# Chunked attention with a gated feed-forward block: upper words of w_in rounded ahead of the addition, first lower products a step later, another order of the beginning

## The chip, the cores and the metric

The kernel runs on one core of one Trainium2 chip. The metric is the time of one execution on the device in microseconds (us); the median of three runs before the change is 371.02 us (370.95 to 371.22). TensorE is called PE here, VectorE DVE, ScalarE ACT, GpSimd POOL and SyncE SP, as in the profile.

## What is computed

Inputs are `q`, `k`, `v` of 4 x 8 heads x 768 x 64, eight memory keys and values a head, and four weights of a gated block.

```
scores = scale * q_c @ [mem_k, k_ctx].T        # chunks of 32 queries, 16 keys left, 8 right
a = exp(scores - max); out = (a / sum(a)) @ [mem_v, v_ctx]
h = relu(x @ w_in)                             # x: the heads side by side, 4 x 768 x 512; w_in 512 x 1024
u, v = h[..., :512], h[..., 512:]
v_s = w_spatial @ normalised(v) + b_spatial
result = (u * v_s) @ w_out
```

All is float32. Every large product is made of three products of rounded words: a matrix is split in an upper word (rounded to fp32r) and a lower word (what is left), and upper x upper, lower x upper and upper x lower are added in PSUM.

## The kernel before, in words

**Attention** goes in 24 units of 128 queries (four chunks of 32), six units a batch, over all eight heads. For unit i: ACT copies the unit's keys into `kmain` (L422), PE makes the scores (L437, `sx<-kmain,q`, called s(i) here), DVE takes the maxima (L494) and subtracts (L498), ACT takes the exponential (L503), DVE sums and inverts (L508, L509, L511, called the denominators), PE transposes (L525), ACT copies (L528, `pT`), PE multiplies with the values (L437, `sx<-vmain,pT`, called a(i), which serves unit i-1 and writes the second half of the tile `sx` of s(i)), DVE scales (L477, `xs`), PE transposes (L541), ACT rounds to the upper word of `x` (L546) and DVE makes the lower word (L550). There is one buffer of `sx`.

**w_in** arrives as float64 words in eight chunks of 128 rows x 512 columns, called w0 to w7 (w0 to w3 are the right half, for `v`; w4 to w7 the left half, for `u`). Of each chunk: ACT scales the high part (L883), DVE shifts and puts the sign in (L892, L893), ACT scales the low part (L888), POOL adds the two in place in the tile `st` (L898, the addition), ACT rounds to the upper word `win_h` (L912), and DVE or POOL subtracts that from `st` for the lower word `win_l` (L916).

**First layer:** `group` (L579 to L581) makes one PSUM tile in four steps, one for each 128 rows of w_in, three products a step. The first group is for the 128 tokens of unit 0. `v` tiles have 512 columns, `u` tiles 384. ACT takes the relu (L603, L641); for `v` DVE takes the statistics (L607, L609, L611). PSUM holds three such tiles.

**Order.** Every piece of work is an operation with a number. `Plan.order` makes a list of them, and `emit` then moves single operations behind others by the table `MOVES`; each engine runs its operations in the order of that list, and what it waits for follows from who wrote or read a tile last in that same list. So a move can also turn a wait round: where rounding stands behind the addition in the list it reads the sum, and where it stands ahead, it reads the tile before the sum is written into it and the addition waits for it. `IDLES` puts idle matmuls of the identity (L277, into a PSUM tile that nobody reads) behind given operations, each 128 x 128 in two instructions. `order` itself puts one more behind a gap that it foresees.

**Loads** stand on SP's queue (L306) in a fixed order: `q`, `k` of units 0 and 1, w0, values, w1 to w3, `q`, `k` of units 2 and 3, values, w4, values, w5 to w7, values, `q`, `k` of units 4 and 5. A load waits for an earlier one by a pace that `transfer` sets, and for the buffer that it fills.

Of the kernel before, what the change touches and what calls it, by code (L numbers as in the profile page):

```python
# [37 lines left out]
)  # L38
IDLES = ((87, 5), (92, 4), (95, 2), (104, 29), (132, 1))
# [7 lines left out]
class Plan:  # L47
# [123 lines left out]
    def emit(self):  # L171
# [5 lines left out]
        for n in order:  # L177
            self.ops[n][2]()
            if n in idles:
                self.idle(idles[n])  # L180
# [3 lines left out]
def tile_chunked_attention_gmlp(  # L184
# [22 lines left out]
    nc = tc.nc  # L207
# [890 lines left out]
```

## Time and profile before

| | |
|---|---|
| median of 3 runs | 371.02 us |
| the profiled execution | 369.22 us |
| its span, first to last instruction | 367.4 us |
| PE busy | 354.0 us (96%) |
| DVE busy | 288.8 us (79%) |
| ACT, POOL busy | 186.2 us (51%), 155.8 us (42%) |
| granted clock of PE | 0.9 or more in every slice of the page |

A timeline row gives the start in us, the duration in us, the engine, the line, the operation with what it writes and reads, its size and count, and in square brackets the idle time of the engine ahead of it with what ended it. A row with several instructions gives the time from the first to the last. PE's durations overlap: the next matmul starts before the last one's end.

### The profile page before, as it was taken

Reading aid. Unit: us, or ns where it says so; the run is one execution under the profiler, and the core shown is the slowest. Engines: PE = TensorE matmul, PEld = TensorE weight load, DVE = VectorE, ACT = ScalarE, POOL = GpSimd, SP = SyncE. Lnnn points to the kernel's source line nnn. Section 1 sums busy time; section 2 is a strip of 40 time slices with the busy share of each in tenths; the row PEclk is TensorE's granted clock in tenths of the full one; section 3 lists DMA queues with packets and bytes.
Section 4 is the critical chain, followed back from the end, with each engine's and each line's share of the span. In section 5 each row is a group of like instructions: output and inputs, shape, how many; then the busy total and the mean of one; then the engine's idle time right before and its main releaser. Section 6 shows DMA issues by size and latency. Waiting matters only on the chain.

```text
span 367.4 us, 11909 instructions
## 1 busy us (share of the span) xinstructions
PE 354.0 (96%) x5026; PEld 328.2 (89%) x5026; DVE 288.8 (79%) x480; ACT 186.2 (51%) x334; POOL 155.8 (42%) x154
## 2 busy tenths in 40 slices
PE   2899999999999999999999999999999999999995
PEld 2787888988988989889889899999999999999995
DVE  3799977669659589485598697898899995997793
ACT  3668553645555355554383447346524742753361
POOL 6254643366377057820024184931295034304330
PEclk9999999999999999999999999999999999999999
DMA  8999988884797894978553619304730582230015
GB/s 210 272 234 247 218 266 251 260 259 145 223 253 208 230 268 158 250 169 286 185 167 115 242 70 337 139 1 144 235 140 2 185 242 90 79 123 15 2 43 172
DMA packets 47557, 65.52 MB, mean 178 GB/s; under 512 B 4496, under 2 KB 38928, under 8 KB 47504
## 3 DMA queue, kind: packets, MB, share of 16 engines
q1 hardware_dynamic: 46848, 64.44, 59.1%
q8 instruction: 39, 0.64, 0.8%
q10 hardware_dynamic: 656, 0.33, 0.3%
q14 instruction: 14, 0.11, 0.1%
HBM read 45.88 MB, written 18.87 MB: 176 GB/s over the span
## 4 chain that ended last, share of the span: by engine, by line
PE 87%; DMA 5%; DVE 4%; ACT 2%; issue 1%; SPq 0%; ACTq 0%
PE y L729 23%; PE f L729 16%; PE f L579 12%; PE f L580 11%; PE f L581 11%; PE sx L437 9%; DMA k<-in_k_dram 3%; PE pt L525 3%; PE xt L541 3%; DMA vmain<-in_v_dram 2%; DVE st L893 1%; DVE st L892 1%; DVE p L498 1%; DVE mx L494 1%; DVE ve L611 0%
## 5 line engine op out<-in xcount | busy, mean ns | idle before, releaser
L729 PE MATMUL y<-wsp,op 128*128 128x384 f32 x288 | 52.2, 336 | 0.0
L729 PEld LDWEIGHTS y<-wsp,op 128*128 128x128 f32 x288 | 49.9, 188 | 0.0
L579 PE MATMUL f<-x,win_h 128*128 128x384 f32 x128 | 45.9, 359 | 0.0
L783 POOL TENSOR_TENSOR ug<-st,ug 128x384 f32<-128x384 f32 x24 | 34.7, 1461 | 20.8 <-DVE st L775 16.7
L581 PE MATMUL f<-x,win_h 128*128 128x384 f32 x128 | 43.1, 337 | 0.0
L580 PE MATMUL f<-x,win_l 128*128 128x384 f32 x128 | 43.0, 336 | 0.0
L789 POOL TENSOR_TENSOR st<-st,bias 128x384 f32<-128x384 f32 x14 | 17.2, 1233 | 58.0 <-ACT st L769 39.1
L579 PE MATMUL f<-win_h,x 128*128 128x512 f32 x96 | 41.1, 428 | 0.0
L729 PE MATMUL f<-wsp,op 128*128 128x384 f32 x216 | 39.6, 336 | 0.0
L580 PE MATMUL f<-win_h,x 128*128 128x512 f32 x96 | 38.1, 397 | 0.6 <-DVE x L550 0.2
L709 DVE TENSOR_TENSOR op<-sm,op 128x768 fp32r<-128x768 f32 x32 | 34.7, 1087 | 4.0 <-ACT op L706 3.6
L581 PE MATMUL f<-win_l,x 128*128 128x512 f32 x96 | 37.6, 392 | 0.0
L729 PEld LDWEIGHTS f<-wsp,op 128*128 128x128 f32 x216 | 37.6, 188 | 0.0
L729 PE MATMUL y<-wout,op 128*128 128x256 f32 x288 | 35.8, 279 | 0.0
L615 POOL TENSOR_TENSOR rstd<-ve,mhalf 128x1 f32<-128x1 f32 x24 | 14.3, 598 | 49.6 <-DVE ve L611 49.2
L477 DVE TENSOR_TENSOR xs<-sx,rec 128x512 f32<-128x512 f32 x24 | 16.5, 688 | 23.8 <-PE sx L437 23.8
L729 PEld LDWEIGHTS y<-wout,op 128*128 128x128 f32 x288 | 34.8, 188 | 0.0
L706 ACT CAST op<-sm 128x768 fp32r<-128x768 f32 x32 | 26.4, 838 | 14.5 <-DVE sm L692 13.8
L437 PEld LDWEIGHTS sx<-kmain,q 64*32 64x32 f32 x1536 | 17.1, 107 | 14.0 <-issue 11.4
L603 ACT ACTIVATE st<-f 128x512 f32<-128x512 f32 x24 | 14.4, 598 | 28.5 <-PE f L581 28.1
L437 PE MATMUL sx<-kmain,q 64*32 64x64 f32 x1536 | 21.1, 227 | 7.2 <-ACT kmain L422 7.2
L416 POOL COPY vmain<-memv 8x1024 f32<-8x1024 f32 x22 | 23.9, 1090 | 9.8 <-PE sx L437 7.6
(86 smaller groups left out, 776.4 us busy)
## 6 DMA issues: line engine op xcount, KB each, us to landing
vmain<-in_v_dram SPq DMA_DIRECT2D x48, 128.0 KB
u_far<-uo SPq DMA_DIRECT2D x32, 192.0 KB
vn_far<-st SPq DMA_DIRECT2D x24, 256.0 KB
vr<-vn_far SPq DMA_DIRECT2D x8, 768.0 KB
ug<-u_far SPq DMA_DIRECT2D x16, 384.0 KB
q<-in_q_dram SPq DMA_DIRECT2D x11, 512.0 KB
vmain<-in_v_dram SPq DMA_DIRECT2D x47, 96.0 KB
out_dram<-ot SPq DMA_DIRECT2D x33, 128.0 KB
```

What stands on the lines that cost most here:

```text
L416: ins = {"DVE": nc.vector, "POOL": nc.gpsimd}[eng].tensor_copy(to, of)
L437: ins = nc.tensor.matmul(o, w_, m, start=True, stop=True, skip_group_check=True)
L477: nc.vector.tensor_tensor(xs.rearrange("p t r d -> p r t d"), t_["sx", i][:, :, 1], rec.rearrange("p t r -> p r t").unsqueeze(3).broadcast ...
L579: nc.tensor.matmul(o, lh, rh, start=(j == 0), stop=False)
L580: nc.tensor.matmul(o, ll, rh, start=False, stop=False)
L581: nc.tensor.matmul(o, lh, rl, start=False, stop=(j == len(pairs) - 1))
L603: nc.scalar.activation(alloc("st", s, [P, DH], F32), t_["f", n], AF.Relu)
L706: nc.scalar.copy(half(0), of())
L709: nc.vector.tensor_tensor(half(1), of(), half(0).bitcast(F32), op=ALU.subtract)
L729: nc.tensor.matmul(o, x, y, start=first and m == 1, stop=m == 3 * chunks, skip_group_check=True)
L783: nc.gpsimd.tensor_tensor(g, t_[st(x)], g, op=ALU.mult)
L789: {"DVE": nc.vector, "POOL": nc.gpsimd}[eng].tensor_tensor(a, a, bias[:, 1], op=ALU.add)
```

## The change

`LOWER` says at which step of the first group (`n == 0`) the products with the lower words `win_l` are made: none at the first step, that of w0 at the second, that of w1 at the third, those of w2 and w3 at the fourth. The twelve products of the group stay the same, the order in which they are added changes. The idle matmuls may now be small (32 columns, 64 rows), and 41 of `IDLES` become 33 large and 8 small ones. `MOVES` gets some 90 more pairs ahead of the old ones, all for operations of the first 45 us. Every other line is the same, moved by 10 to 16 lines.

```diff
 MOVES = (
-    (1035, 934), (1027, 975), (1036, 941), (1028, 948), (1037, 1028), (1038, 1037), (963, 951), (964, 950),
...
+    (22, 21), (23, 22), (24, 23), (25, 24), (32, 25), (39, 32), (11, 39), (86, 85), (87, 86), (88, 87), (89, 88),
...
-IDLES = ((87, 5), (92, 4), (95, 2), (104, 29), (132, 1))
+IDLES = ((87, (5, 128)), (95, (5, 128)), (104, (4, 128), (5, 128)), (102, (14, 128)), (594, (8, 32)))
...
+LOWER = ((), (0,), (1,), (2, 3))
...
-        idles = dict(IDLES)
+        idles = {n: how for n, *how in IDLES}
         for n in order:
             self.ops[n][2]()
-            if n in idles:
-                self.idle(idles[n])
+            for how in idles.get(n, ()):
+                self.idle(*how)
...
-    def busy(k):
-
-        for _ in range(k):
-            nc.tensor.matmul(idle, ident, ident, start=True, stop=True)
+    def busy(k, w):
+        for j in range(k):
+            if w < P:
+                c = j % 4 * w
+                nc.tensor.matmul(idle[c:c + w, 0:w], ident[0:64, 0:w], ident[0:64, 0:w], start=True, stop=True)
+            else:
+                nc.tensor.matmul(idle[:, 0:P], ident, ident, start=True, stop=True)
...
-                nc.tensor.matmul(o, lh, rl, start=False, stop=(j == len(pairs) - 1))
+                for i in (LOWER[j] if n == 0 else (j,)):
+                    lh, _, _, rl = pairs[i]()
+                    nc.tensor.matmul(o, lh, rl, start=False, stop=(i == len(pairs) - 1))
```

**ACT around the copies of the keys of units 2 and 3.** Before, `st_333`, `st_266`, `st_391`, `st_400` are the tiles of w1, w0, w2, w3 and `big_282` the words of w3:

```order
L912 CAST win_h_108<-st_333 128x512
L883 ACTIVATE st_400<-big_282 128x512
L888 ACTIVATE big_282<-big_282 128x512
L912 CAST win_h_108<-st_266 128x512
L912 CAST win_h_108<-st_391 128x512
L422 COPY kmain0_147<-k_384 128x20x32
L422 COPY kmain1_148<-k_384 128x20x32
L912 CAST win_h_108<-st_400 128x512
L503 ACTIVATE p_464<-p_464 128x512
```

Now, `st_344`, `st_346`, `st_372` are those of w1, w2, w3, and `big_176`, `big_178` the words of w2 and w3 (w0 is rounded far ahead of this):

```order
L928 CAST win_h_108<-st_344 128x512
L904 ACTIVATE big_176<-big_176 128x512
L542 COPY pT_383<-pt_353 128x512
L928 CAST win_h_108<-st_372 128x512
L436 COPY kmain0_147<-k_377 128x20x32
L928 CAST win_h_108<-st_346 128x512
L436 COPY kmain1_148<-k_377 128x20x32
L904 ACTIVATE big_178<-big_178 128x512
L517 ACTIVATE p_442<-p_442 128x512
```

The rounding of w2 and the low part of w3 now stand behind the first copy of the keys.

**DVE from the maxima of unit 2 on.** Before (`win_l_109<-st_400` is the lower word of w3, `st_508` is w4, `stats_606` the statistics of the first group):

```order
L494 TENSOR_REDUCE mx_459<-sx_419 128x8
L498 TENSOR_TENSOR p_464<-sx_419,mx_459 128x2x4x64
L916 TENSOR_TENSOR win_l_109<-st_400,win_h_108 128x512
L477 TENSOR_TENSOR xs_504<-sx_419,rec_338 128x2x4x64
L508 TENSOR_REDUCE den_518<-p_464 128x8
L509 TENSOR_TENSOR den_518<-den_518,eps_103 128x8
L511 RECIPROCAL rec_521<-den_518 128x8
L892 TENSOR_SCALAR st_508<-st_508 128x512
L893 SCALAR_TENSOR_TENSOR st_508<-big_405,st_508 128x512
L607 BN_STATS stats_606<-st_568 128x6
```

Now (`st_346` is w2, `st_372` w3, `st_506` w4):

```order
L508 TENSOR_REDUCE mx_440<-sx_405 128x8
L512 TENSOR_TENSOR p_442<-sx_405,mx_440 128x2x4x64
L932 TENSOR_TENSOR win_l_109<-st_346,win_h_108 128x512
L932 TENSOR_TENSOR win_l_109<-st_372,win_h_108 128x512
L491 TENSOR_TENSOR xs_523<-sx_405,rec_391 128x2x4x64
L908 TENSOR_SCALAR st_506<-st_506 128x512
L909 SCALAR_TENSOR_TENSOR st_506<-big_398,st_506 128x512
L522 TENSOR_REDUCE den_533<-p_442 128x8
L523 TENSOR_TENSOR den_533<-den_533,eps_103 128x8
L525 RECIPROCAL rec_536<-den_533 128x8
L623 BN_STATS stats_603<-st_514 128x6
```

The lower word of w2, which stood ahead of the maxima, now stands behind the subtraction, so that one more operation lies between the maxima of unit 2 and the statistics of the first group.

**PE from s(2) on.** Before:

```order
L437 MATMUL sx<-kmain_147,q 32x64 x32
L579 MATMUL f<-win_h,x 128x512
L580 MATMUL f<-win_h,x 128x512
L581 MATMUL f<-win_l,x 128x512
L579 MATMUL f<-win_h,x 128x512
L580 MATMUL f<-win_h,x 128x512
L581 MATMUL f<-win_l,x 128x512
L437 MATMUL sx<-vmain,pT 32x64 x32
```

Now:

```order
L451 MATMUL sx<-kmain_147,q 32x64 x32
L593 MATMUL f<-win_h,x 128x512
L594 MATMUL f<-win_h,x 128x512
L593 MATMUL f<-win_h,x 128x512
L594 MATMUL f<-win_h,x 128x512
L597 MATMUL f<-win_l,x 128x512
L593 MATMUL f<-win_h,x 128x512
L594 MATMUL f<-win_h,x 128x512
L597 MATMUL f<-win_l,x 128x512
L451 MATMUL sx<-vmain,pT 32x64 x32
```

s(2) still stands ahead of the first product, and three steps of the first group instead of two stand ahead of a(2).

**DVE at the addition of w6.** Before, `st_615`, `st_642`, `st_679` are the tiles of w5, w6, w7 and `big_506`, `big_524` the words of w6 and w7:

```order
L916 TENSOR_TENSOR win_l_109<-st_615,win_h_108 128x512
L892 TENSOR_SCALAR st_642<-st_642 128x512
L893 SCALAR_TENSOR_TENSOR st_642<-big_506,st_642 128x512
L508 TENSOR_REDUCE den_688<-p_649 128x8
L509 TENSOR_TENSOR den_688<-den_688,eps_103 128x8
L511 RECIPROCAL rec_691<-den_688 128x8
L607 BN_STATS stats_703<-st_664 128x6
L609 BN_AGGR mvar_705<-stats_703 128x2
L611 TENSOR_TENSOR ve_707<-mvar_705,eps_103 128x1
L892 TENSOR_SCALAR st_679<-st_679 128x512
L893 SCALAR_TENSOR_TENSOR st_679<-big_524,st_679 128x512
```

Now `st_632`, `st_668`, `st_665` are those of w5, w6, w7 and `big_490`, `big_495` the words of w6 and w7:

```order
L932 TENSOR_TENSOR win_l_109<-st_632,win_h_108 128x512
L908 TENSOR_SCALAR st_668<-st_668 128x512
L909 SCALAR_TENSOR_TENSOR st_668<-big_490,st_668 128x512
L908 TENSOR_SCALAR st_665<-st_665 128x512
L909 SCALAR_TENSOR_TENSOR st_665<-big_495,st_665 128x512
L623 BN_STATS stats_694<-st_670 128x6
L625 BN_AGGR mvar_696<-stats_694 128x2
L627 TENSOR_TENSOR ve_698<-mvar_696,eps_103 128x1
L932 TENSOR_TENSOR win_l_109<-st_668,win_h_108 128x512
L522 TENSOR_REDUCE den_762<-p_649 128x8
```

The shifts of w7 now stand right behind those of w6; before, the denominators and the statistics stood between them.

## Rows read from the trace of the kernel before

**Rows 1.** Waits of PE, whole span: who waited for whom, us, times, longest.

```profile
PE sx L437 <- ACT kmain L422: 7.2, 3, 6.7
...
PE sx L437 <- ACT uo L641: 0.3, 1, 0.3
```

**Rows 2.** Busy time by stretch: length, engines, granted clock, DMA share, GB/s.

```profile
23.20:42.90 19.70, 18.97 (x392) 15.03 (x392) 18.49 (x35) 13.18 (x24) 9.64 (x10) 1.00 1.00 231
...
48.80:367.40 318.60, 314.70 (x4199) 294.56 (x4199) 249.98 (x409) 156.37 (x284) 129.73 (x121) 1.00 0.55 169
```

**Rows 3.** Chain of waits, 23 to 50 us: the two loads ahead of s(4).

```profile
28.75 6.89 DMA vmain<-in_v_dram
...
35.65 6.49 DMA k<-in_k_dram
```

**Rows 4.** Waits of SP's queue, 16 to 24 us.

```profile
SPq L306 <- DMA k<-in_k_dram: 2.1, 1, 2.1
```

**Rows 5.** Timeline of SP at the end of that wait.

```profile
22.44 0.30 SPq L306 DMA_DIRECT2D vmain<-in_v_dram  x1
```

**Rows 6.** Timeline of PE, 6 to 50 us.

```profile
7.84 2.36 PE L277 MATMUL idle<-ident 128*128 128x128 f32 x10
...
11.41 1.06 PE L277 MATMUL idle<-ident 128*128 128x128 f32 x8
13.10 0.85 PE L437 MATMUL sx<-vmain,pT 64*32 64x64 f32 x64 [0.63 <-DVE st L893]
...
16.41 6.64 PE L277 MATMUL idle<-ident 128*128 128x128 f32 x58
23.23 0.86 PE L437 MATMUL sx<-kmain,q 64*32 64x64 f32 x64 [0.18 <-ACT kmain L422]
...
42.94 0.86 PE L437 MATMUL sx<-kmain,q 64*32 64x64 f32 x64 [0.32 <-ACT kmain L422]
...
48.76 0.89 PE L437 MATMUL sx<-vmain,pT 64*32 64x64 f32 x64 [0.34 <-ACT uo L641]
```

**Rows 7.** Timeline of ACT, 9 to 49 us: a rounding, the copies of the keys.

```profile
21.82 0.62 ACT L912 CAST win_h<-st 128x512 fp32r<-128x512 f32 x1 [0.47 <-POOL st L898]
22.45 1.35 ACT L422 COPY kmain<-k 128x640 f32<-128x640 f32 x2
...
42.16 1.35 ACT L422 COPY kmain<-k 128x640 f32<-128x640 f32 x2 [2.50 <-DMA k<-in_k_dram]
```

**Rows 8.** Timeline of POOL, 9 to 49 us.

```profile
23.84 1.69 POOL L898 TENSOR_TENSOR st<-st,big 128x512 uint32<-128x512 uint32 x1 [0.63 <-DVE st L893]
...
34.66 1.29 POOL L916 TENSOR_TENSOR win_l<-st,win_h 128x512 fp32r<-128x512 f32 x1
```

**Rows 9.** Timeline of DVE, 16 to 49 us.

```profile
22.11 1.65 DVE L893 SCALAR_TENSOR_TENSOR st<-big,st 128x512 uint32<-128x512 uint32 x1
...
25.00 0.69 DVE L498 TENSOR_TENSOR p<-sx,mx 128x512 f32<-128x512 f32 x1
26.21 0.69 DVE L916 TENSOR_TENSOR win_l<-st,win_h 128x512 fp32r<-128x512 f32 x1 [0.53 <-ACT win_h L912]
...
27.42 0.68 DVE L508 TENSOR_REDUCE den<-p 128x8 f32<-128x512 f32 x1
...
28.46 0.38 DVE L892 TENSOR_SCALAR st<-st 128x512 uint32<-128x512 uint32 x1
...
29.51 0.69 DVE L607 BATCH_NORM_STATS2 stats<-st 128x6 f32<-128x512 f32 x1
...
30.93 0.68 DVE L550 TENSOR_TENSOR x<-xt,x 128x512 fp32r<-128x512 f32 x1
...
35.40 1.11 DVE L916 TENSOR_TENSOR win_l<-st,win_h 128x512 fp32r<-128x512 f32 x1 [0.21 <-ACT win_h L912]
...
46.27 0.69 DVE L508 TENSOR_REDUCE den<-p 128x8 f32<-128x512 f32 x1 [0.16 <-ACT p L503]
...
47.96 0.69 DVE L494 TENSOR_REDUCE mx<-sx 128x8 f32<-128x512 f32 x1
```

38 rows, old and new, of the table MOVES are left out of this document.

## The prediction

> **What bounds the kernel now.** I read the table of busy times first, then PE's waits, then busy time by stretch, then the timelines of the stretch that the diff touches.
>
> PE is busy for 354.0 of 367.4 us, so the end moves only if PE starts its unbroken run at another time, or if that run gets other work. From 48.8 us on PE is busy for 314.70 of 318.60 us [rows 2]. The operations there stand in the same order in both kernels, so nothing there is a term of the sum. PE's waits name the keys: 7.2 us in three waits for the copies into `kmain`, 6.7 of them at the start [rows 1]. What is left of them are 0.18 us ahead of s(2) and 0.32 us ahead of s(4); the last wait ahead of the run is 0.34 us at a(5), which starts at 48.76 [rows 6]. The question is how a(5) moves.
>
> Two things set it. The first is the **loads**. From 23.2 to 42.9 us the DMA engines are busy with a share of 1.00 [rows 2], and the chain into s(4) is two loads end to end, values to 35.64 and keys from 35.65 to 42.14 [rows 3]; ACT copies these keys at 42.16 [rows 7]. The keys of units 2 and 3 let SP go on at 22.44 after a wait of 2.1 us [rows 4, 5], ACT copies them at 22.45 [rows 7], s(2) starts at 23.23 [rows 6]. The second is **DVE**, busy for 18.49 of 19.70 us between s(2) and s(4), nearly as full as PE with 18.97 [rows 2]. At a(5) the profile names ACT's relu (L641, 0.3 us) [rows 1], but DVE's maxima L494 of unit 5 end at 47.96 + 0.69 = 48.65, just ahead of 48.76 [rows 6, 9], and a(5) writes the tile whose scores those maxima read. I take DVE as the later one.
>
> **Ahead of s(2).** The idle matmuls go from 82 large instructions to 66 and 16 small ones, and most of the steps of w0 to w3 are sorted anew. All of it ends at s(2), which waits for keys that land at 22.44. The loads stand in the same order on SP with the same waits, so this part costs 0 at s(2); its cover is the wait for the keys, and without it each idle instruction that is left would cost 114 ns (6.64 / 58) [rows 6]. The lower word of w1, ahead of the maxima on DVE, has to be through by 24.3; the shifts of w2 and w3 that took 1.65 us instead of 0.69 there [rows 9] now come earlier. Cost 0.
>
> **The gain side.** Between s(2) and a(2) there is one step more on PE, which fills time that PE stood there. The twelve products are the same twelve. Two idle instructions ahead of the first step of the second group go, 0.23 us at 114 ns. The eight small ones are new in the first `u` tile: two instructions each, at the 13 ns of a small matmul of s(2) (0.86 / 64) 0.2 us, at 114 ns 1.8 us [rows 6]. They are nearest to the former and lie ahead of s(4), where PE waited 0.32 us for the keys: 0, and 0.2 if that cover is gone. None of this can bring s(4) ahead of its keys. Behind s(4) PE runs the same operations, so the whole change can gain at most the wait at a(5): **0.34 us**, which gives 370.7.
>
> **The loss side.** Rounding w2 now waits behind the first copy of the keys on ACT, and POOL's addition of w2 waits for the rounding, since it overwrites what the rounding reads. Queued behind it on POOL is the addition of w3; who waits for both is DVE's two lower words.
>
> - One copy ends at 22.45 + 1.35/2 = 23.12, the rounding (0.62) ends at about 23.75 [rows 7].
> - POOL's addition starts then. One took 1.69 us while DVE worked on a lower word; a subtraction of the same size took 1.29 without such company ahead of it [rows 8]. DVE is at the maxima and the subtraction of unit 2 here, and the subtraction kept its 0.69 us beside the addition that ran from 23.84 [rows 8, 9]. So I take 1.29: w2 to 25.05, w3 to 26.35.
> - DVE ends the subtraction at 25.69 [rows 9]. The lower word of w2 comes next, while POOL is in the middle of w3. At 35.40 the same operation met POOL's of 34.66: it took 1.11 and ended at 36.51, 0.56 behind POOL's end of 35.95 [rows 8, 9]. Here it then ends at 26.35 + 0.56 = 26.91 and the next starts 0.09 earlier, as at 36.42: **26.82**.
> - The next is the lower word of w3, which started at 26.21 before [rows 9]. From it to the end of the lower word of `x` (31.61) the list holds the same operations in both kernels: lower word, `xs`, the denominators (1.04, 27.42 to 28.46), the shift of w4 (1.05), the statistics (1.42, 29.51 to 30.93) [rows 9], now with the shift ahead of the denominators. So all of it moves by 26.82 - 26.21 = **+0.61 us**.
>
> Bounds of this term: if the lower word of w2 isn't held up at all, the sum of w3 is still there only at 26.35, and DVE is 0.14 later than before; if both additions take 1.69, it is 0.61 + 0.80 = 1.41. I take 0.61, since the row at 35.40 is the same pair of operations in the same phase.
>
> Then the same DVE operations follow up to the maxima of unit 5. DVE has two idle gaps on the way, 0.21 at 35.40 and 0.16 at 46.27 [rows 9]; both are waits for ACT, which follows DVE there, so I let them stay. If both absorbed their length, 0.24 of the 0.61 would be left. The keys at 42.16 don't help: the maxima of unit 4 were already waiting for DVE and not for s(4). The 0.34 us at a(5) is no cover either, since it is DVE that ends it. Sum: a(5) from 48.76 to about 49.37, the profiled execution from 369.22 to 369.8. The median of before is 1.80 us above that execution; I carry the difference over: 371.02 + 0.6 = **371.6**.
>
> SP is moved past as well: the loads of w5 to w7 wait for buffers that POOL's additions free. The third of them is issued ahead of the values load of 28.75 [rows 3], and the addition of w3 ends at 26.35 by the above: 2.4 us of cover, cost 0; cut off, each microsecond would be one at s(4).
>
> [...]
>
> **The rivals.**
> 1. *The delay doesn't reach PE.* The gaps absorb it, or the lower word of w2 isn't held up and a(5) gains part of its 0.34 us: 370.7 to 371.2. For it: the profile names ACT at a(5). Against: DVE has 1.2 us of idle time in nearly 20. Chance 0.15.
> 2. *A second collision, slower.* Its place is POOL's addition of w6 against DVE's shift of w7, which now stands right behind the shift of w6; before, denominators and statistics lay between. If ACT's low part of w6 ends before DVE starts L909 of w7 (L893 before), POOL gets in first and L909 waits. The row at 22.11 gives the price, 1.65 - 0.69 = 0.96 [rows 9]: 371.6 + 0.96 = 372.6. Against: ACT is busy enough there that its low part may well come later. Chance 0.20.
> 3. *PE's clock falls.* [...] Now the run at 11.41 goes, so that PE stands still from there to about 13.10, 1.7 us where the longest wait was 0.63, and 28 idle instructions ahead of s(2) replace 58 and end, at 114 ns each, about 1.6 us ahead of it. [...] Chance 0.06.
> 4. *The keys come earlier*, because the new order frees a buffer or paces a load sooner than the list shows; s(2) or s(4) then starts some 1 us ahead: 370.0. Against it stands the DMA share of 1.00 [rows 2]. Chance 0.06.
>
> **How the numbers follow.** 371.6 has 0.53, with its own range from 371.2 (+0.14 to +0.24) to 372.0 (one of the two additions at 1.69). A measurement of this kernel can tell about 0.2%, 0.74 us, from no change. Faster, below 370.3: rival 4, 0.06. Within: rival 1 and most of the forecast, 0.15 + 0.45 = 0.60. Slower, above 371.76: rivals 2 and 3 and the upper end of the forecast, 0.20 + 0.06 + 0.08 = 0.34. The range runs from the 0.34 us of gain to rival 2, 370.7 to 372.6, and leaves out rivals 3, 4 and the far side of 2.
>
> **What the changed profile would show.** Right: copies of keys at 22.4 and 42.2 as before; POOL's additions of w2 and w3 at 23.8 and 25.1; DVE's first L932 after the subtraction 1.1 to 1.4 us long, ending at 26.9; the lower word of `x` ending at 32.2; a(5) at 49.4. Wrong: copies of the keys elsewhere (rival 4, and the sum has no ground); a lower word of 0.69 at 25.6 (the term is 0.14 or less); a(5) at 48.8 or before with DVE's chain later (rival 1, the bound was ACT); an L909 of some 1.65 us behind w6 (rival 2); the granted clock under 1 at s(2) (rival 3).

## The result, and the profile after

The changed kernel takes 373.74 us (median of 22 runs) against 371.37 for the kernel before (22 runs). The ratio is 1.0053 with a 95% interval of 1.0031 to 1.0075: slower by 2.0 us (1.2 to 2.8); the difference of the means is 1.6 (0.7 to 2.5). Ratios, differences of means and their intervals, here and below, leave out the runs that took over 1.5% longer than the fastest of their kernel; medians and counts take in all. The forecast was 371.6 with a range of 370.7 to 372.6, so the direction is right and the size is not.

The profiled execution of the changed kernel has a span of 370.1 us, 2.7 more than before. (The profiled one of before, 369.22 us, was faster than all but one of the 156 other runs of that kernel, so what is measured against it is measured against a good run.) The timeline of PE from a(1) to a(5):

```profile
13.37 0.85 PE L451 MATMUL sx<-vmain,pT 64*32 64x64 f32 x64 [1.16 <-DMA vmain<-in_v_dram]
...
19.03 3.29 PE L291 MATMUL idle<-ident 128*128 128x128 f32 x28
23.74 0.86 PE L451 MATMUL sx<-kmain,q 64*32 64x64 f32 x64 [1.43 <-ACT kmain L436]
...
44.34 0.85 PE L451 MATMUL sx<-kmain,q 64*32 64x64 f32 x64 [0.41 <-issue]
...
50.78 0.96 PE L451 MATMUL sx<-vmain,pT 64*32 64x64 f32 x64 [1.00 <-ACT uo L657]
```

These rows answer to [rows 6]. a(5) starts 2.02 us later (48.76 before), which accounts for most of the 2.7. PE now stands 1.43 us ahead of s(2) (0.18 before) and 1.16 ahead of a(1) (0.63 before). The stretch behind a(5) is 0.7 us longer (319.3 against 318.6); in the profiles below it varies from 318.5 to 325.9 with waits that the profile calls issue, and I leave that 0.7 open.

ACT's copy of the keys of units 2 and 3, against [rows 7]; POOL's additions of w2 and w3, of w6, and a copy of values at the end, against [rows 8]:

```profile
22.97 0.72 ACT L436 COPY kmain<-k 128x640 f32<-128x640 f32 x1 [0.87 <-DMA k<-in_k_dram]
```

```profile
24.29 2.58 POOL L914 TENSOR_TENSOR st<-st,big 128x512 uint32<-128x512 uint32 x2 [3.40 <-ACT win_h L928]
...
38.88 1.36 POOL L914 TENSOR_TENSOR st<-st,big 128x512 uint32<-128x512 uint32 x1 [1.75 <-ACT big L904]
...
48.45 1.04 POOL L430 COPY vmain<-memv 8x1024 f32<-8x1024 f32 x1
```

DVE against [rows 9]: the two lower words, the scaling behind them, the shift of w7, the scaling ahead of s(4), the denominators and the maxima ahead of a(5):

```profile
25.98 2.05 DVE L932 TENSOR_TENSOR win_l<-st,win_h 128x512 fp32r<-128x512 f32 x2
27.95 0.68 DVE L491 TENSOR_TENSOR xs<-sx,rec 128x512 f32<-128x512 f32 x1
...
39.12 1.68 DVE L909 SCALAR_TENSOR_TENSOR st<-big,st 128x512 uint32<-128x512 uint32 x1
...
43.55 0.69 DVE L491 TENSOR_TENSOR xs<-sx,rec 128x512 f32<-128x512 f32 x1
...
48.50 1.02 DVE L523 TENSOR_TENSOR den<-den,eps 128x8 f32<-128x8 f32 x1
...
49.99 0.69 DVE L508 TENSOR_REDUCE mx<-sx 128x8 f32<-128x512 f32 x1
```

The keys came 0.52 us later. Counted from their copy, the scaling stands at 4.98 us; in the kernel before it was 26.82 - 22.45 = 4.37. That is the +0.61 that the prediction has. L909 of w7 takes 1.68 us, and the denominators' small addition behind POOL's copy 1.02: so there were further collisions. Counted from the copy of the keys, a(5) stands at 27.81 us, and at 26.31 before: of the 2.02, 0.52 is the keys' and 1.50 comes behind their copy.

The run list holds something that this one profile does not show: 16 of the 22 runs have a mean granted clock of PE of 0.9965 or less and take 374.8 us (median); the other six, the profiled one among them, take 371.9.

### The profile page after: what moved, and what is told of

It reads as the page before. It is cut to its first block, busy times and chain, and to the rows that moved or that the text cites. A ratio compares the mean times of both kernels' runs of the same rounds, so it can differ in the third digit from the quotient of the medians.

```text
span 370.1 us, 11910 instructions
## 1 busy us (share of the span) xinstructions
PE 352.6 (95%) x5026; PEld 326.5 (88%) x5026; DVE 287.3 (78%) x480; ACT 186.5 (50%) x334; POOL 154.2 (42%) x154
## 4 chain that ended last, share of the span: by engine, by line
PE 88%; DMA 6%; DVE 3%; ACT 1%; issue 1%; SPq 1%; ACTq 0%
PE y L745 23%; PE f L745 16%; PE f L593 13%; PE f L594 12%; PE f L597 12%; PE sx L451 8%; DMA big<-in_moe_w_in_dram 3%; PE xt L555 3%; PE pt L539 2%; DMA k<-in_k_dram 2%; SPq L320 1%; DVE win_l L932 1%; DVE ve L627 0%; DMA out_dram<-st 0%; DVE x L564 0%
## 5 line engine op out<-in xcount | busy, mean ns | idle before, releaser
L745 PEld LDWEIGHTS y<-wsp,op 128*128 128x128 f32 x288 | 49.9, 188 | 0.1
L657 ACT ACTIVATE uo<-f 128x384 f32<-128x384 f32 x32 | 15.6, 492 | 24.1 <-PE f L597 18.1
```

What stands on the lines that cost most here:

```text
L657: op("ACT", act(HT), lambda: nc.scalar.activation(alloc("uo", i, [P, HT], F32), t_["f", n], AF.Relu), r=[("f", n)], w=[("uo", i)], rank=rank)
L745: nc.tensor.matmul(o, x, y, start=first and m == 1, stop=m == 3 * chunks, skip_group_check=True)
```

## The experiments

Three theories stood against each other. D: DVE's collisions with POOL make a(5) late. K: the new order brings the keys late. C: PE's clock falls, since the change leaves PE idle ahead of a(1) and s(2). The table counts every run of a kernel, twelve a version; "low" is the number of runs whose mean granted clock is 0.9965 or less. The difference is that of the means, against 20 to 35 runs of the kernel before taken at the same time, with a 95% interval from resampling the runs. The last column is a(5) in the profile, counted from the copy of the keys of units 2 and 3.

| kernel | low | median us | mean, less the kernel before | a(5) less keys |
|---|---|---|---|---|
| before, all runs beside the others | 32 of 134 | 371.54 | | 26.31 |
| changed, first 22 runs | 16 of 22 | 373.74 | +1.57 (0.7 to 2.5) | 27.81 |
| again (changed) | 6 of 12 | 372.55 | +0.81 (-0.1 to 1.7) | 29.11, clock low |
| idle_cut | 10 of 12 | 373.63 | +1.90 (1.0 to 2.8) | 30.23, clock low |
| idle_late | 2 of 12 | 372.54 | +0.82 (0.3 to 1.4) | 27.83 |
| idle_first | 1 of 12 | 372.59 | +1.13 (0.3 to 2.1) | 28.02 |
| idle_back | 7 of 12 | 378.09 | +5.54 (4.4 to 6.6) | 27.81 |
| w2_early | 4 of 12 | 372.63 | +0.24 (-0.6 to 1.1) | 27.80 |
| w7_apart | 5 of 12 | 372.19 | -0.36 (-1.3 to 0.5) | 28.54, late keys |
| mend | 4 of 12 | 373.08 | +0.77 (-0.3 to 1.7) | 26.69 |
| mend_all | 2 of 12 | 371.16 | -0.51 (-1.4 to 0.4) | 26.19 |
| lower_only | 4 of 12 | 371.48 | -0.52 (-1.5 to 0.6) | 27.57, late keys |
| before_gap | 2 of 12 | 372.07 | +0.30 (-0.7 to 1.3) | 26.95 |
| before_cut | 10 of 12 | 372.49 | +1.27 (0.1 to 2.4) | 27.24, clock low |
| before_both | 12 of 12 | 373.38 | +0.80 (-0.3 to 2.0) | 27.18, clock low ahead of s(2) |
| before_w2 | 1 of 12 | 372.13 | +0.62 (-0.3 to 1.5) | 26.90 |
| before_w7 | 3 of 12 | 370.83 | -0.53 (-1.7 to 0.7) | 26.09 |

"Late keys" marks profiles in which the keys of units 4 and 5 are copied more than 21 us behind those of units 2 and 3 (19.7 before) and s(4) starts 0.1 us behind their first copy, so that they and not DVE set it. (In idle_cut they are copied 21.35 us behind, but s(4) starts 1.6 us after that copy.) All four profiled runs that are low, again, idle_cut, before_cut and before_both, have their stretch of low clock between 16 and 30 us (down to 0.57 over 2 us in before_cut, to 0.50 in the other three); in the other 13 the granted clock is 1.00 in every stretch from 14 to 30 us and from 48.8 to 367.4.

### The changed kernel again, and its clock

**again** is the changed kernel with nothing edited.

> The changed kernel a second time, nothing edited. Its first profile had the keys of units 2 and 3 copied at 22.97 us (22.45 in the kernel before), the scaling behind DVE's two lower words at 27.95 (26.82), DVE's L909 of w7 1.68 us long, a(5) at 50.78 (48.76) and a mean granted clock of 0.999; over its 22 runs the clock lay between 0.990 and 1.000. Theory D (DVE's chain: two collisions with POOL, 0.6 and 1.0 us, and 0.5 us from the keys): both collisions again, the scaling 4.98 us behind the copy of the keys, a(5) between 50.2 and 50.8. Theory K (the new order brings the keys late): the copy again at 22.9 or later; if it was chance, at 22.3 to 22.7. Theory C (PE's clock falls because PE stands idle for 1.43 us ahead of s(2)): the runs with a mean clock of 0.995 or less are the majority and take some 2 us more than those at 0.999 and 1.000, and a profile of such a run shows the low stretch right behind 23 us.

Half of its runs were low, and the mean of its runs is 0.8 us above the kernel before, where the first 22 had 1.6. a(5) came at 53.55 us, where 50.2 to 50.8 was expected. Its profile is of a low run. ACT's copy of the keys and PE's s(2), then busy time by stretch (the last three numbers are the granted clock, the DMA share and GB/s):

```profile
24.44 0.72 ACT L436 COPY kmain<-k 128x640 f32<-128x640 f32 x1 [1.85 <-DMA k<-in_k_dram]
```

```profile
25.22 1.19 PE L451 MATMUL sx<-kmain,q 64*32 64x64 f32 x64 [2.64 <-ACT kmain L436]
```

```profile
22.00:24.00 2.00, 0.58 (x6) 0.38 (x4) 1.93 (x5) 0.59 (x1) 0.00 (x0) 1.00 1.09 196
24.00:26.00 2.00, 0.78 (x58) 0.79 (x63) 0.13 (x1) 1.56 (x3) 0.24 (x1) 0.70 0.84 183
26.00:28.00 2.00, 2.00 (x33) 1.54 (x20) 1.52 (x3) 0.94 (x3) 2.00 (x2) 0.50 1.00 172
28.00:30.00 2.00, 2.00 (x69) 1.38 (x68) 1.47 (x2) 0.76 (x2) 0.31 (x1) 0.95 0.93 203
```

The keys were copied 1.5 us later than in the first profile, PE was busy for 0.58 of the 2 us ahead, and its granted clock is 0.70 from 24 to 26 us and 0.50 from 26 to 28. s(2) takes 1.19 instead of 0.86 us, and a(5) comes 1.3 us later than at full clock, counted from the keys. The clock is back at 0.95 from 28 to 30 us, after PE worked through the 2 us ahead.

Theory K is not borne out as a rule of the order: over all 17 profiles the copy of the keys lies between 21.59 and 24.44 us, the order of the loads being the same in all, and both the earliest (mend) and the latest (again) belong to the changed order. The mean is 23.11 in the seven profiles built on the kernel before and 23.11 in the ten built on the changed one; 22.45, from which the prediction reckoned, is the earliest of the seven.

**idle_cut** and **idle_late** move twelve idle instructions between the run ahead of s(2) and the small ones later, the count kept:

```diff
-IDLES = ((87, (5, 128)), (95, (5, 128)), (104, (4, 128), (5, 128)), (102, (14, 128)), (594, (8, 32)))
+IDLES = ((87, (5, 128)), (95, (5, 128)), (104, (4, 128), (5, 128)), (102, (8, 128)), (594, (14, 32)))    # idle_cut
+IDLES = ((87, (5, 128)), (95, (5, 128)), (104, (4, 128), (5, 128)), (102, (20, 128)), (594, (2, 32)))    # idle_late
```

> The changed kernel, the count of idle instructions kept, twelve of them moved the other way: 16 ahead of s(2) instead of 28, so that the run ends at about 20.9 us and PE stands for 2.4 us or more ahead of s(2). Theory C: 9 or more of 12 runs below 0.9965, median 374 to 375, and in the profile a granted clock near 0.8 in the stretch from 20 to 30 us. Theory D: no change from the changed kernel, full clock in half of the runs or more.

> The changed kernel with as many idle instructions as it has, twelve of them moved: the run ahead of s(2) has 40 instead of 28 and ends at about 23.7 us instead of 22.3, and 4 small ones are left behind the first step of the u tile instead of 16. So far the changed kernel had a mean granted clock of 0.9965 or less in 22 of 34 runs (median 374.7 us; 371.9 in the others), the kernel before in 7 of 35 (374.7; 370.9). Theory C (PE's clock falls where PE stands idle for long ahead of s(2), longer when the keys land late): 2 to 4 of 12 runs below 0.9965, the median down by 1 to 2 us to about 372. Theory D (DVE's chain alone, and the clocks a matter of the chip's hour): the share stays at half to two thirds and the median at 372.5 to 373.7. Theory I (idle instructions more or fewer shift PE's later instructions and it waits for those, which cost the version with 34 more of them 5 us): nothing of that here, since the count is kept; PE's waits for issue behind 50 us stay at a few tenths.

Ten of 12 were low with the shorter run, 22 of 34 as changed, 2 of 12 with the longer one. In the profile of idle_cut PE stood 3.21 us ahead of s(2):

```profile
18.76 1.95 PE L291 MATMUL idle<-ident 128*128 128x128 f32 x16
23.92 1.18 PE L451 MATMUL sx<-kmain,q 64*32 64x64 f32 x64 [3.21 <-ACT kmain L436]
```

In idle_late it stood for 0.70 us, though the keys came later than in the first profile:

```profile
18.80 4.63 PE L291 MATMUL idle<-ident 128*128 128x128 f32 x40
24.13 0.86 PE L451 MATMUL sx<-kmain,q 64*32 64x64 f32 x64 [0.70 <-ACT kmain L436]
```

So in this order the number of idle matmuls ahead of s(2) decides in how many runs the clock falls. It also sets the time: the mean of idle_cut is 1.08 us above that of idle_late (0.3 to 1.9), and both were run at the same time. idle_cut's median of 373.6 lies just under the expected 374 to 375. But idle_late stays 0.82 us above the kernel before (0.3 to 1.4) with hardly a low run: theory C does not make the whole difference.

**idle_first** leaves the run ahead of s(2) at 28 and puts ten large instructions into the gap ahead of a(1), where the kernel before had eight:

```diff
+IDLES = ((87, (5, 128)), (92, (5, 128)), (95, (5, 128)), (104, (4, 128), (5, 128)), (102, (14, 128)), (594, (3, 32)))
```

> The changed kernel with the count of idle instructions kept and ten of the sixteen small ones replaced by ten large ones in the earlier gap, between the first transposes and a(1), where PE stood for 1.2 to 1.7 us and where the kernel before had eight. The run ahead of s(2) stays at 28. Theory C1 (only the gap right ahead of s(2) counts): 6 or more of 12 runs below a mean clock of 0.9965, as the changed kernel (22 of 34). Theory C2 (what PE did earlier counts too, since the kernel before with a gap of 1.8 us ahead of s(2) fell in only 2 of 12): 1 to 4 of 12, median 371.5 to 372.5.

One of 12 was low. For the clock, filling the earlier gap does as much as filling the later one; the median of 372.6 is at the upper end of what was expected.

**before_gap, before_cut** and **before_both** give the gaps to the kernel before (with the lines of the change that read `IDLES` and make small instructions, left out here):

```diff
-IDLES = ((87, 5), (92, 4), (95, 2), (104, 29), (132, 1))
+IDLES = ((87, (5, 128)), (92, (4, 128)), (95, (2, 128)), (104, (22, 128)), (132, (1, 128)), (594, (7, 32)))    # before_gap
+IDLES = ((87, (5, 128)), (92, (4, 128)), (95, (2, 128)), (104, (15, 128)), (132, (1, 128)), (594, (14, 32)))   # before_cut
+IDLES = ((87, (5, 128)), (95, (2, 128)), (104, (22, 128)), (132, (1, 128)), (594, (11, 32)))                   # before_both
```

> The kernel before with its run of idle matmuls ahead of s(2) cut from 58 to 44 instructions, so that it ends at about 21.4 us instead of 23.05, and 14 small ones behind the first step of the u tile (the count is kept). Theory C: 6 or more of 12 runs below 0.9965 and a median 1 to 2.5 us above the kernel before. Theory D: the clocks as in the kernel before, the time within 0.3 us of it.

> The kernel before with its run of idle matmuls ahead of s(2) cut from 58 to 30 instructions, so that it ends at about 20 us and PE stands for some 3 us ahead of s(2); 28 small ones behind the first step of the u tile keep the count. Theory C: 9 or more of 12 runs below 0.9965, the median 2 us or more above the kernel before, and in the profile a low granted clock from s(2) on, with a(5) 2 us or more later at the same landing of the keys. If the order and not PE's gap makes the clock fall: no more than 4 of 12.

> The kernel before with both of the changed kernel's gaps on PE and nothing else of it: the eight idle instructions between the first transposes and a(1) gone, the run ahead of s(2) cut from 58 to 44, and 22 small ones behind the first step of the u tile that keep the count. With the second gap alone 2 of 12 runs fell below a mean clock of 0.9965; the changed kernel with the first gap filled fell in 1 of 12, with neither filled in 22 of 34. Theory C2 (the two gaps together make the clock fall): 6 or more of 12 below 0.9965, the median 1 us or more above the kernel before. If something else of the new order is needed: no more than 3 of 12.

The expectation for before_gap failed: with only the later gap (1.78 us ahead of s(2) in its profile, at full clock) 2 of 12 were low and the time did not move clear of noise. A much longer one made 10 of 12 low, but the median came 1.0 us above the kernel before and a(5) 0.9 later, where 2 us were expected of both. The two gaps together made 12 of 12 low, as expected; the time rose by 0.8 us, with an interval that holds zero (-0.3 to 2.0). In the profile of before_both the clock is low between the two places, not behind the second:

```profile
16.00:18.00 2.00, 2.00 (x10) 2.00 (x11) 1.90 (x5) 1.08 (x3) 0.00 (x0) 0.50 0.98 295
18.00:20.00 2.00, 2.00 (x14) 2.00 (x14) 1.14 (x3) 2.00 (x4) 1.29 (x1) 0.66 0.89 267
```

There idle matmuls take the loss: the run of 44 took 5.87 us instead of the 5.08 of before_gap, and s(2) waited for the keys all the same (0.35 us), so this fall cost nothing there. a(5) is 0.87 us later by another wait, which before_gap has too, without a low clock: PE's products break off at 31 us, in before_gap put down to issue and in before_both to an operation of ACT on other data, and DVE's scaling waits for them. before_gap first, then before_both:

```profile
31.49 0.32 PE L440 MATMUL sx<-kmain,q 64*32 64x64 f32 x8 [1.27 <-issue]
```

```profile
32.64 0.69 DVE L480 TENSOR_TENSOR xs<-sx,rec 128x512 f32<-128x512 f32 x1 [0.60 <-PE sx L440]
```

```profile
32.15 0.85 PE L440 MATMUL sx<-vmain,pT 64*32 64x64 f32 x64 [1.53 <-ACT big L891]
```

```profile
33.06 0.69 DVE L480 TENSOR_TENSOR xs<-sx,rec 128x512 f32<-128x512 f32 x1 [0.70 <-PE sx L440]
```

So in before_both the gaps are shown to make the clock fall, and what the falls cost is not. In the profile of again it was the products behind s(2) that took the loss (4.01 us from s(2) to a(2), 2.83 in the changed kernel's first profile). In which share of the runs the clock falls at which place the runs don't tell, since only a profiled one has the clock by stretch. Within one version low runs have a mean some 2 us above the others (changed kernel 2.1, kernel before 2.4); loads that land late in them may be a part of that.

**idle_back** was the first try at filling both gaps, with 104 idle instructions instead of 82 (22 more; a later expectation says 34, a slip):

```diff
+IDLES = ((87, (5, 128)), (92, (5, 128)), (95, (5, 128)), (104, (4, 128), (5, 128)), (102, (20, 128)), (594, (8, 32)))
```

> The changed kernel with idle matmuls in the two gaps that it leaves on PE: ten more instructions between the first transposes and a(1), and forty in place of 28 ahead of s(2), which should end at about 23.7 instead of 22.3. Theory C: nearly all runs at a clock of 0.999 or 1.000, and the median falls by 1 to 2 us against the changed kernel in the same call. Theories D and K: a(5) stays at 50.2 to 50.8 and the times stay within 0.5 us of the changed kernel's.

It lost 5.3 us, far behind the place of the edit. Its profile has waits of PE in the middle of a row of products, put down to nothing but issue:

```profile
179.25 0.60 PE L539 MATMUL pt<-ident,p 128*128 128x128 f32 x4 [1.07 <-issue]
...
184.61 0.33 PE L451 MATMUL sx<-vmain,pT 64*32 64x64 f32 x11 [2.01 <-issue]
```

idle_late, with the same run of 40 ahead of s(2) but the count kept, has 0.7 and 0.4 us of such waits and not this loss, and neither has mend_all below, with both gaps filled and the count kept. So the loss goes with the number of PE's instructions ahead of that place (104 idle ones against 82). The expectation, nearly all runs at full clock, failed too: 7 of 12 are low with both gaps filled. The profiled run is not one of them, and where the clock falls in them stays open. Why PE waits for issue there no run shows.

### DVE's collisions, one by one

**before_w2** puts the order of w2 alone into the kernel before, with the deferred lower products (the loop that reads `LOWER` is left out here); **lower_only** has the deferred products and nothing else:

```diff
+LOWER = ((), (0,), (1,), (2, 3))                                                    # lower_only, before_w2
-    (1499, 1505),
+    (1499, 1505), (44, 41), (20, 19), (37, 114), (36, 37), (43, 36), (38, 119),     # before_w2
```

> The kernel before with the one edit that the products with the lower words in the first group come a step later (none, w0, w1, w2 and w3); order and idle matmuls as before. All theories: within 0.4 us of the kernel before, since the same twelve products stand between s(2) and the statistics of the first group; a share of runs below 0.9965 like that of the kernel before.

> The kernel before with the lower products a step later and with that part of the new order that holds back w2: the rounding of w2 behind the first copy of the keys on ACT, POOL's additions of w2 and w3 behind it, the lower word of w2 behind the subtraction of unit 2 on DVE. Idle matmuls as before. Theory D: additions at about 1.3 and 2.6 us behind the copy of the keys, the two lower words 2.0 us long together, the scaling behind them 5.0 us behind the copy of the keys (4.37 in the kernel before), a(5) 0.6 us later than in the kernel before at the same landing of the keys, and the median of the runs at 0.9965 or more 0.3 to 0.9 us above those of the kernel before. Theory C: the share of runs below 0.9965 as in the kernel before, 1 to 5 of 12. If the collision costs nothing at PE: no difference.

lower_only is not to be told from the kernel before (+0.43, -1.0 to 2.0); its profile is set by late keys. In before_w2 POOL's two additions, DVE's two lower words, and a(5):

```profile
24.56 2.56 POOL L901 TENSOR_TENSOR st<-st,big 128x512 uint32<-128x512 uint32 x2 [1.19 <-ACT win_h L915]
```

```profile
26.25 2.02 DVE L919 TENSOR_TENSOR win_l<-st,win_h 128x512 fp32r<-128x512 f32 x2
28.19 0.68 DVE L478 TENSOR_TENSOR xs<-sx,rec 128x512 f32<-128x512 f32 x1
```

```profile
50.14 0.85 PE L438 MATMUL sx<-vmain,pT 64*32 64x64 f32 x64 [0.60 <-ACT uo L644]
```

The keys were copied at 23.24. The additions start 1.32 us behind that, the scaling stands at 4.95, a(5) at 26.90: 0.59 more than before, where 0.6 was expected. The interval of the runs' mean (+0.62, -0.3 to 1.5) is too wide to confirm it by itself.

**w2_early** rounds w2 ahead of the keys again, **w7_apart** puts the denominators and statistics back between the shifts, in the changed kernel:

```diff
-    (1499, 1505),
+    (1499, 1505), (37, 44),               # w2_early
+    (1499, 1505), (138, 79), (79, 575),   # w7_apart
```

> The changed kernel with the rounding of w2 ahead of the copy of the keys on ACT instead of behind it; everything else in the same order. Theory D: POOL's additions of w2 and w3 start 0.9 us or more sooner, DVE's two lower words take 1.3 instead of 2.05 us and the scaling behind them comes 4.2 instead of 4.98 us behind the copy of the keys; a(5) 0.6 to 0.8 us sooner, unless the lower word of w1 now meets the addition of w2. Theory K: no change in the keys. Theory C: the times hardly move.

> The changed kernel with the denominators of unit 3 and the statistics of the second group put back between DVE's shifts of w6 and w7, as before. Theory D: L909 of w7 takes 0.7 instead of 1.68 us and a(5) comes 0.8 to 1.0 us sooner, at 49.4 to 49.9; the times fall by the same. Theory C: L909 shortens too, but the times hardly move, since the clock makes them.

w2_early shortened the two lower words to 1.46 us and brought the scaling to 4.52 behind the keys, but a(5) stayed at 27.80: the shift of w4 then started 0.2 us later than DVE was free, an addition met the statistics' small operation, and the denominators ran into POOL's copy as before. w7_apart cleared L909 as expected (0.69 us), but a(5) came at 51.08 and not at the expected 49.4 to 49.9: in its profile the keys of units 4 and 5 were copied only at 44.12 and set s(4), so the profile decides nothing. Its runs lie 1.2 us below those of again (0.1 to 2.2), taken at the same time; mend's, below, don't confirm that, so what the shift of w7 costs is not settled.

**mend** is w7_apart with the idle matmuls of idle_late, **mend_all** has both orders mended and both gaps filled:

```diff
+IDLES = ((87, (5, 128)), (95, (5, 128)), (104, (4, 128), (5, 128)), (102, (20, 128)), (594, (2, 32)))                   # mend
+    (1499, 1505), (138, 79), (79, 575),                                                                                 # mend
+IDLES = ((87, (5, 128)), (92, (5, 128)), (95, (2, 128)), (104, (4, 128), (5, 128)), (102, (18, 128)), (594, (2, 32)))   # mend_all
+    (1499, 1505), (138, 79), (79, 575), (37, 44),                                                                       # mend_all
```

> The changed kernel with two things mended: the run of idle matmuls ahead of s(2) with 40 instructions instead of 28 (4 small ones left, the count kept), and the denominators of unit 3 and the statistics back between DVE's shifts of w6 and w7. Theories C and D together: 1 to 4 of 12 runs below 0.9965, L909 of w7 0.7 us long, median 371.3 to 372.0, against 372.5 with the idle matmuls alone; that is 0 to 0.6 us above the kernel before, the collision of w2 and w3 being left. Theory D alone would want 0.9 us from the shifts, theory C alone nothing beyond 372.5.

> The changed kernel with all three causes taken away: ten large idle instructions in the gap ahead of a(1), 36 instead of 28 ahead of s(2) and fewer elsewhere (the count kept), the rounding of w2 ahead of the copy of the keys, and denominators and statistics back between the shifts of w6 and w7. Theories C2 and D: 0 to 3 of 12 runs below 0.9965, a(5) 26.3 to 26.8 us behind the copy of the keys (27.8 in the changed kernel), the mean within 0.5 us of the kernel before and 0.8 to 2 us below the changed kernel's 373.7. If it is clearly faster than the kernel before, the deferred lower products are worth something by themselves.

In mend a(5) stands at 26.69 behind the keys, 1.14 less than in idle_late; in mend_all at 26.19, as in the kernel before (26.31). Of mend_all, the copy of the keys and a(5):

```profile
23.52 1.35 ACT L436 COPY kmain<-k 128x640 f32<-128x640 f32 x2 [1.05 <-DMA k<-in_k_dram]
```

```profile
49.71 0.86 PE L451 MATMUL sx<-vmain,pT 64*32 64x64 f32 x64
```

mend's runs don't follow its profile: 371.3 to 372.0 was expected, and the median is 373.1 against 372.5 in idle_late, the means being equal within noise (372.4 and 372.5). mend_all's mean is 0.5 us below the kernel before with an interval that holds zero: with the orders and the gaps mended nothing is left of the loss (the mean is 1.6 us below that of the changed kernel, 0.8 to 2.4), and a gain over the kernel before is not shown.

**before_w7** puts the shift of w7 behind that of w6 in the kernel before:

```diff
-    (1499, 1505),
+    (1499, 1505), (78, 71), (79, 72),
```

> The kernel before with DVE's shift of w7 moved right behind that of w6, and ACT's scaling of w7 behind that of w6; idle matmuls as before. Theory D: L893 of w7 takes some 1.7 us where it took 0.69, since POOL adds w6 then, and a(5) comes 27.2 to 27.5 us behind the copy of the keys of units 2 and 3 instead of 26.3, if the keys of units 4 and 5 are no later than 20 us behind that copy. The median of the runs at full clock 0.3 to 1.0 us above the kernel before's. If the shift finds no addition beside it: no change.

The collision came and the delay did not. DVE's L893 of w7, and the three small operations that follow:

```profile
38.53 1.68 DVE L893 SCALAR_TENSOR_TENSOR st<-big,st 128x512 uint32<-128x512 uint32 x1
...
40.85 0.17 DVE L509 TENSOR_TENSOR den<-den,eps 128x8 f32<-128x8 f32 x1
...
44.28 0.25 DVE L611 TENSOR_TENSOR ve<-mvar,eps 128x1 f32<-128x1 f32 x1
...
47.34 0.17 DVE L509 TENSOR_TENSOR den<-den,eps 128x8 f32<-128x8 f32 x1
```

In the kernel before these three took more, and POOL's instructions lay beside them, ending at 39.01, 44.17 and 47.48, at most 0.03 us ahead of theirs:

```profile
38.20 0.84 DVE L509 TENSOR_TENSOR den<-den,eps 128x8 f32<-128x8 f32 x1
...
43.36 0.83 DVE L611 TENSOR_TENSOR ve<-mvar,eps 128x1 f32<-128x1 f32 x1
...
46.99 0.50 DVE L509 TENSOR_TENSOR den<-den,eps 128x8 f32<-128x8 f32 x1
```

So the shift lost 0.99 us and the small operations won 0.67 + 0.58 + 0.33 = 1.58; a(5) stands at 26.09, a little better than before. So one collision can't be priced alone. I add up, from the maxima of unit 2 to a(5), what shifts, lower words and small additions of DVE take beyond 0.69 and 0.17 us: 2.49 us in the kernel before, 3.84 in the changed kernel, 2.17 in mend, 1.47 in mend_all, 3.22 in before_w2, 1.52 in before_w7. The step from 2.49 to 3.84 is 1.35, near the 1.50 us by which a(5) is later. But the sum is not the whole account. mend_all loses 1.0 us less than the kernel before, and its a(5) is only 0.12 sooner; DVE waits 0.46 us for ACT on the way. before_gap and before_both lose as much as the kernel before (2.45 and 2.48) and have a(5) 0.64 and 0.87 later, by the wait for PE shown above. And idle_first, whose L909 of w7 takes 0.69 us and which loses 2.9, has a(5) at 28.02, since DVE waits 0.21 and 0.67 us for ACT's roundings. The waits of DVE count as well as what it loses, and a(5) of the old order stands at 26.3 to 27.2 in profiles without late keys, at 27.8 to 28.0 in those of the changed order at full clock and with no more than the idle matmuls or w2 moved.

## Why the prediction was wrong

- **The loss at w2: right, in mechanism and size.** Forecast +0.61 us; the changed kernel's scaling is 0.61 later counted from the keys, and before_w2 has 0.59 at a(5). POOL's additions take 1.29 each as taken, and DVE's next operation comes where the row at 35.40 [rows 9] put it.
- **"Ahead of s(2) ... cost 0": the step that failed.** The cover that I named, the wait for the keys, hides the time of those instructions and not what they do for PE's clock (10 of 12 runs low with 16 of them ahead of s(2), 2 of 12 with 40); the term was put at nothing. The fall of the clock stood there as rival 3, with both gaps named, and got a chance of 0.06; it came in 22 of 34 runs, against 32 of 134 before. What a fall costs no row of the kernel before shows; in the profile of again a(5) came 1.3 us later than at full clock, and over the runs the size is less certain. idle_cut and idle_late differ by 1.08 us (0.3 to 1.9) at 10 and 2 low runs of 12, by an estimate 1.6 us for each further run that falls. At that price the changed kernel's falls cost some 0.8 us (1.6 times the difference of 22/34 and 3/24) against idle_first and idle_late; the difference of the means measured there is 0.5 us (373.12 against 372.64), with an interval of -0.2 to 1.1.
- **One trace was taken for the load times.** The prediction held the keys at 22.44 and gave the clock a small chance because idle matmuls then ended 1.6 us ahead. The keys are copied up to 2 us later in other profiles, and the time for which PE stands grows with that (1.43 us with the copy at 22.97, 2.64 at 24.44).
- **The collision at w7: underrated, and it is not an event by itself.** Rival 2 had 0.20 and 0.96 us. ACT's low part ended in time (POOL's addition of w6 starts at 38.88, L909 at 39.12), L909 took 0.99 more, and mend against idle_late shows 1.1 us at a(5), though their times don't (means 372.4 and 372.5). But before_w7 shows the same collision at no cost, and idle_first a late a(5) without it. I had priced the collisions that the diff names and no others; the small operations, which I took at their length before, changed with the place of POOL's (the denominators' addition ahead of a(5) took 0.50 us before, 1.02 in the changed kernel, 0.17 in before_w7).
- **s(4) held by its keys: not so in every run.** In the changed kernel's first profile s(4) starts at 44.34, behind DVE's scaling (43.55 to 44.24), though the keys were copied at 41.92. In two of the profiles (lower_only, w7_apart) the keys came so late that they set s(4) again, and a delay of DVE then costs less. This, and the good run from which the 26.31 comes, fit a rest without the clock that is smaller than the 1.5 us of the two profiles: idle_first and idle_late together lie 0.84 us above the kernel before (0.4 to 1.3), where nearly all runs keep the clock. That is near what was forecast for w2 alone, but by luck: the collisions behind w2 are in it too.
- **The gain side and the loads' order: right.** lower_only moved nothing that can be seen, the loads are issued in the same order, and no version was found faster by more than its uncertainty.

The runs divide the loss only roughly. All runs of the changed kernel together lie 1.3 us above the kernel before (0.8 to 1.9), where the first 22 gave 1.6 by the means and 2.0 by the ratio. Of the 1.3 the clock has 0.5 to 0.8 us by the two ways above, and as much is left for DVE and whatever else the new order costs. The runs that aren't low, taken alone, lie 0.55 us above those of the kernel before (0.1 to 1.0).

## What to carry to other kernels

The idle matmuls hid here behind a wait for a load and still had a job: 10 of 12 runs were low with 16 of them ahead of s(2), 2 of 12 with 40. Before one is moved or dropped, price PE's clock over the whole spread of that load's landing (2.9 us here) and not at the one time that a trace shows, and look at earlier gaps together with the one ahead of the wait (2 of 12 runs low in before_gap, 12 of 12 in before_both). When two engines collide, add up everything that the waiting engine loses over the stretch, small operations and its waits too, since moving one collision moved the others here (in before_w7 the shift lost 0.99 us and the small operations won 1.58). Take no single profile as the reference: look where its time lies among the other runs. And keep the count of idle instructions while testing where they stand: with 22 more, idle_back lost 5.3 us.

## What the runs showed of the hardware

- An addition of 8 columns, 0.17 us alone, took 1.02 us on DVE beside POOL's copy of values (48.50 to 49.52 against 48.45 to 49.49): it ended 0.03 us behind POOL's instruction. So a short operation was lengthened too. For the large operations the end lies 0.56 us behind POOL's in both kernels (36.51 against 35.95, and 40.80 against 40.24), 0.13 less than a whole operation (0.69).
- Gaps ahead of s(2) stood in runs at full clock and in runs that fell (1.78 us in before_gap, 1.85 in w2_early and 1.43 in the changed kernel's first profile, all at full clock; 2.64 in again, at 0.50 behind it); where an earlier gap stood as well 22 of 34 runs fell in the changed kernel, 12 of 12 in before_both, 4 and 5 of 12 in w2_early and w7_apart; with one of the two filled 1 of 12 fell in idle_first, 2 in idle_late and before_gap, 4 in mend; with a later gap of 4.08 us alone (before_cut) it was 10 of 12.
- With twenty-two idle instructions more, PE's waits for issue behind a(5) come to 5.0 us (0.72 at 68.2 to 2.01 at 184.6); the changed kernel has 0.2, and with the count kept the most was 2.0 (before_w2).
- ACT's copy of the keys of units 2 and 3, whose load has the same place in the queue, varied by 2.9 us over 17 profiled executions (21.59 to 24.44).
